# Four exponentials that stay in PSUM: steps 89, 91, 93 and 95 of an attention loop on one Trainium2 core

## The chip, the cores and the metric

One core of one Trainium2 chip runs the whole program. The metric is the device time of one execution in microseconds (us), smaller is better. The engines are TensorE (PE: matmuls, and PEld: loading their stationary operand), VectorE (DVE), ScalarE (ACT), GpSimd (POOL) and SyncE (SP, which issues most DMAs). SBUF is the working memory, PSUM the memory that matmuls write to.

## What is computed

Three blocks in a row, of which the change touches the first:

```python
# attention, batch 2, 8 heads, 768 tokens, head size 64; a query sees keys of its own cluster only
scores = np.where(mask, q @ k.T / 8, -1e9)
attn = np.exp(scores - scores.max(-1)); attn /= attn.sum(-1)
x = attn @ v
# then: Fourier mixing over tokens and channels, layer norm, a ReLU MLP (512 -> 2048 -> 512)
# then: an MLP with a convolution along the tokens and a sigmoid gate (512 -> 1024 -> 512)
```

## The kernel before

**The attention loop.** There are 16 heads of 6 tiles with 128 keys each, so 96 steps; a step n has all 768 queries of one tile. For a step, `score_exp` (L556) makes the scores t in PSUM with four matmuls and ScalarE writes their exponential p (128x768, f32) to SBUF. To keep precision, p is handed on as two 16-bit parts in one tile p16: `prob_hi` (L568) casts p to f16, `prob_lo` (L575) subtracts that part from p again. `attn_v` (L582) then multiplies both parts with v, in 18 small matmuls, of which the first two read the high part only and the other 16 need the low part as well.

**Who does what.** The cast is ScalarE's except in even steps above 87 and in step 95, where it is VectorE's. The subtraction is VectorE's in the steps of `LO_ON_DVE` (L24), which hold the odd steps from 87 on, and GpSimd's in the others. So in the last steps VectorE casts 88, 90, 92, 94 and 95 and subtracts 89, 91, 93 and 95, and GpSimd subtracts 88, 90, 92 and 94.

**Order and buffers.** Every engine takes its instructions in the order of the program. The loop at L739 does in pass n: the row maxima of step n+8 (none after step 95), the cast of step n-1, scores and exponential of step n, the subtraction of step n-1, the product with v of step n-3, and then extra work that tables (`pre`, `aft`, `post`, `fill`) hang into the pass: layer norm of the first half (`un`), the weights of the first MLP step (`firstEH`, `firstEL`, `firstYsH`, `firstYsL`), a small conversion for later (`cw`, `craw`, L898). Scores, row maxima and transposes take turns in three PSUM slots of two banks (`slot`, L318). p has three buffers, p16 four. In the last steps t91 takes the slot of t89, t94 that of t91, t95 that of t92, and t93 that of a transpose (`unT`).

**After the loop.** The first MLP starts (L882). Its matmuls (`up`, `acc`; L78 to L80) stand on TensorE behind the last product with v, and VectorE's conversions and splits of the weights (L281 to L286, L780, L795) stand behind the scaling of the last attention output (L598 to L603), which needs that product too.

Of the kernel before, what the change touches and what calls it, by code (L numbers as in the profile page):

```python
# [10 lines left out]
F32 = mybir.dt.float32  # L11
# [4 lines left out]
AF = mybir.ActivationFunctionType  # L16
# [4 lines left out]
B, H, S, D = 2, 8, 768, 64  # L21

DFT_LOADS = (20, 32)
LO_ON_DVE = {n for n in range(87) if n % 12 in (1, 2, 7, 11)} | set(range(87, 96, 2))  # L24

AHEAD = 4
AHEAD_STEPS = [12 * q + n for q in range(4) for n in (17, 17, 18, 18, 22)]
C = 16
DM = 512
DFF1, DFF2 = 2048, 1024  # L30
# [12 lines left out]
def tile_net(ctx, tc, qk, v, cen, w12, w34, conv, dft, odd, out):  # L43
    nc = tc.nc
    V, A, G, T = nc.vector, nc.scalar, nc.gpsimd, nc.tensor
# [16 lines left out]
    cbias = cp.tile([128, 1], F32, name="cbias")  # L62
    V.memset(cbias, float(P_SHIFT * np.log(2.0)))

    def pool(ctx_, name, bufs=1, side="left"):
        return ctx_.enter_context(tc.tile_pool(name=name, bufs=bufs, side=side, reuse_waits="tile"))
# [168 lines left out]
    def norm(b, bank, lp):  # L235

        X = U[:, 6 * b:6 * b + 6, :]
        stats, ys, os = {}, {}, {}

        def stat(t):  # L240
            if b not in uns:
                uns[b] = up_[b].tile([128, 2, 4, S], F32R, tag="un", bufs=1, name=f"un{b}")
            st = lp.tile([128, 6], F32, tag="st", bufs=2, name=f"st{b}{t}")
            V.bn_stats(st, X[:, t])
            mv = lp.tile([128, 2], F32, tag="mv", bufs=3, name=f"mv{b}{t}")
            V.bn_aggr(mv, st)
            rs = lp.tile([128, 1], F32, tag="rs", bufs=3, name=f"rs{b}{t}")
            V.tensor_scalar(rs, mv[:, 1:2], 1e-6, None, ALU.add)
            stats[t] = (mv, rs)

        def root(t):
            rs = stats[t][1]
            G.tensor_tensor(rs, rs, half[:, 2:3], ALU.pow)

        def scale(t):
            mv, rs = stats[t]
            y = ys[t] = lp.tile([128, DM], F32, tag="y", bufs=1, name=f"y{b}{t}")
            V.tensor_scalar(y, X[:, t], mv[:, 0:1], rs, ALU.subtract, ALU.mult)

        def swap(t):  # L260
            o = os[t] = bank(f"unT{b}{t}").rearrange("p (c n) -> p c n", c=4)
            for c in range(4):
                T.transpose(o[:, c], ys[t][:, 128 * c:128 * c + 128], ident)
            A.copy(uns[b][:, 0, :, 128 * t:128 * t + 128], o)

        def low(t):
            tk = slice(128 * t, 128 * t + 128)
            V.tensor_sub(uns[b][:, 1, :, tk], os[t], f32(uns[b][:, 0, :, tk]))

        return stat, root, scale, swap, low  # L270
# [4 lines left out]
    def from64(dst, raw):  # L275


        w0, w1 = (raw.rearrange("p (n t) -> p n t", t=2)[:, :, i] for i in range(2))
        d = dst.bitcast(I32)
        return (  # L280
            lambda: V.tensor_scalar(d, w1, 3, 0x3FFFFFFF, ALU.logical_shift_left, ALU.bitwise_and),  # L281
            lambda: V.scalar_tensor_tensor(d, w1, -0x40000000, d, ALU.bitwise_and, ALU.bitwise_or),
            lambda: A.activation(f32(w1), f32(w1), AF.Square),
            lambda: V.scalar_tensor_tensor(dst.bitcast(U32), w0.bitcast(U32), 29, dst.bitcast(U32),
                                           ALU.logical_shift_right, ALU.bitwise_or),
            lambda: V.scalar_tensor_tensor(dst, f32(w1), LEAST, dst, ALU.is_ge, ALU.mult),  # L286
        )
# [22 lines left out]
    with ExitStack() as actx:  # L310
        ap = pool(actx, "ap")
# [6 lines left out]
        def slot(name):  # L318
            turn[0] = (turn[0] + 1) % 3
            return ps.tile([128, 2, 512], F32, tag=f"s{turn[0]}", bufs=1, name=name)  # L320
# [37 lines left out]
        t = slot("warm_up")  # L358
# [22 lines left out]
        A.copy(W[64:128, :, 16:32], pwv[:, :, 1])  # L381
        desc = ep.tile([128, C], F16, name="desc")
        for c in range(C):
            G.memset(desc[:, c:c + 1], float(C - c))
        V16s = []
        for i in range(2):
            t = ap.tile([128, NT, 2, 130], F16, name=f"V16_{i}")
# [10 lines left out]
        def prep_sims(m):  # L398
            raw = raws[m]
            sm = sims[m] = first_bank("sim1") if m == 1 else slot(f"sim{m}")[:, 0]  # L400
            for t in range(12):
# [4 lines left out]
            V.tensor_reduce(mx, sv, AX.X, ALU.max)  # L406
            eq = eqs[m] = ep.tile([128, 24, C], F16, tag="eq", bufs=1, name=f"eq{m}")
            V.tensor_tensor(eq.rearrange("p (h g) c -> p h g c", h=2), sv,
                            mx.unsqueeze(3).to_broadcast([128, 2, 12, C]), ALU.is_equal)

        def prep_first(m, eng=G):
            eng.tensor_tensor(eqs[m], eqs[m], desc.unsqueeze(1).to_broadcast([128, 24, C]), ALU.mult)

# [140 lines left out]
        probs, p32s = {}, {}  # L554

        def score_exp(n):  # L556
            h, i = n // 6, n % 6
            X, Y = Xs[h % 3], Ys[h % 3]
            t = slot(f"t{n}")
            sl = slice(128 * i, 128 * i + 128)  # L560
            for c in range(2):
                T.matmul(t[:, c, 0:384], X[:, 1, sl], X[:, 0, 384 * c:384 * c + 384], start=True, stop=False)  # L562
            for c in range(2):
                T.matmul(t[:, c, 0:384], Y[0:98, 1, sl], Y[0:98, 0, 384 * c:384 * c + 384], start=False, stop=True)  # L564
            p = p32s[n] = ap.tile([128, S], F32, tag="p", bufs=3, name=f"p{n}")
            A.activation(p.rearrange("p (c n) -> p c n", c=2), t[:, :, 0:384], AF.Exp, bias=cbias, scale=0.125)  # L566

        def prob_hi(n):  # L568
            p16 = probs[n] = ap.tile([128, 2, S], F16, tag="p16", bufs=4, name=f"p16_{n}")
            if n > 87 and n % 2 == 0 or n == 95:  # L570
                V.tensor_copy(p16[:, 0], p32s[n])
            else:
                A.copy(p16[:, 0], p32s[n])  # L573

        def prob_lo(n):  # L575
            p, p16 = p32s.pop(n), probs[n]
            eng = V if n in LO_ON_DVE else G
            eng.tensor_sub(p16[:, 1], p, p16[:, 0])  # L578

        avs, ds = {}, {}  # L580

# [27 lines left out]
        def at(where, step, *f):  # L609
            where.setdefault(step, []).append(f)  # L610
# [50 lines left out]
        stat, root, scale, swap, low = norm(0, lambda name: slot(name)[:, 0], dp)  # L661
        for i, t in enumerate((0, 3, 1, 4, 2, 5)):
            n = 72 + 3 * i
# [8 lines left out]
        def ahead_start(q):  # L672
# [6 lines left out]
            dst = ahead[q] = t[:, 2560 + 512 * q:3072 + 512 * q]  # L679
            for n, op in zip(AHEAD_STEPS[5 * q:], from64(dst, raw)):  # L680
                at(aft, n, op)
# [9 lines left out]
        for q in range(AHEAD):  # L691
            at(pre, AHEAD_STEPS[5 * q] - 3, ahead_start, q)
            at(pre, AHEAD_STEPS[5 * q + 4] + 1, ahead_store, q)
        for f in range(2):
# [44 lines left out]
        for n in range(-LEAD, 6 * NH + 10):  # L739
            for f in pre.get(n, []):  # L740
                f[0](*f[1:])
            score_max(n + LEAD, mid.get(n, []))
            if 0 <= n - 1 < 6 * NH:
                prob_hi(n - 1)
            if 0 <= n < 6 * NH:
                score_exp(n)
            if 0 <= n - 1 < 6 * NH:
                prob_lo(n - 1)
            if 0 <= n - LAG < 6 * NH:
                attn_v(n - LAG)  # L750
            for f in aft.get(n, []) + post.get(n, []) + fill.get(n, []):
                f[0](*f[1:])
            if n in DFT_LOADS:
                i = DFT_LOADS.index(n)
                G.dma_start(out=DC[:, i], in_=dft[:, i])
            if n == DFT_LOADS[1] + 1:
                G.dma_start(out=OD, in_=odd)
            if n == 6 * NH - 10:
                ectx.close()
                wst.append(pool(ctx, "wst0", side="right"))  # L760
                cvs.append(pool(ctx, "cv", side="right"))
# [219 lines left out]
```

## Time and profile before

| | |
|---|---|
| median of 3 runs | 752.48 us (751.13 to 2342.31) |
| the profiled execution | 750.55 us, of which its span is 748.8 us |
| TensorE busy | 698.7 us, 93% of the span |
| VectorE busy | 536.4 us, 72% |
| ScalarE busy | 345.9 us, 46% |
| GpSimd busy | 271.2 us, 36% |
| the last steps, from the exponential of step 89 to the first matmul of the MLP | 282.6 to 302.0 us |

One of the three runs, 2342.31 us, is far from the other two, 751.13 and 752.48. Shares of the span are averages over stages with different limits; the views below are cut to the last steps of the loop and to what follows them. In a timeline a row is one instruction (or several that follow each other); the bracket at its end says how long the engine was idle before it and which instruction's end released it.

### The profile page before, as it was taken

To read this page: it belongs to the slowest core of one execution; us is meant where nothing else is said; L and a number is where in the kernel's file an instruction comes from. 1 tells how busy PE (TensorE), PEld (TensorE's weight loads), DVE (VectorE), ACT (ScalarE), POOL (GpSimd) and SP (SyncE) were. 2 spreads that over 40 slices of the span, in tenths; PEclk is the share of its full clock that TensorE was granted. 3 is DMA by queue.
4 is the path that set the end of the run, shared out by engine and by line. 5 is a ranking of instruction groups with operands and counts; after the bars stand their busy time and mean duration, and the time that the engine had idled before them with its cause. 6 is when DMAs were issued, how large, how long until landed. Compare 5 with 4: busy or idle time off the path is not lost.

```text
span 748.8 us, 12517 instructions
## 1 busy us (share of the span) xinstructions
PE 698.7 (93%) x5090; PEld 623.2 (83%) x5090; DVE 536.4 (72%) x754; ACT 345.9 (46%) x492; POOL 271.2 (36%) x189
## 2 busy tenths in 40 slices
PE   8898999897998996989999999999999999999996
PEld 6787788786897885878988899999999788898984
DVE  7778989679977998999379937765111268777664
ACT  3576868586466685334234433433222233333321
POOL 8154644455244544131041003222232154443441
PEclk9999999999799999899999999999999999999999
DMA  7637678462533431214104321430000000002002
GB/s 219 173 78 209 184 196 251 107 196 59 157 71 79 92 116 59 98 71 169 57 0 169 116 109 57 168 113 1 1 0 1 1 0 1 1 1 84 1 1 84
DMA packets 19937, 66.47 MB, mean 89 GB/s; under 512 B 2868, under 2 KB 5928, under 8 KB 16808
## 3 DMA queue, kind: packets, MB, share of 16 engines
q1 hardware_dynamic: 19448, 61.93, 28.5%
q0 software_dynamic: 432, 3.75, 1.5%
q8 instruction: 40, 0.66, 0.3%
q14 instruction: 17, 0.14, 0.1%
HBM read 40.94 MB, written 5.77 MB: 62 GB/s over the span
## 4 chain that ended last, share of the span: by engine, by line
PE 48%; DVE 34%; ACT 5%; DMA 4%; POOL 4%; issue 3%; SPq 1%; POOLq 0%; DVEq 0%
PE up L78 5%; DVE m L533 5%; PE up L80 5%; PE up L79 5%; PE acc L80 5%; PE acc L78 5%; PE acc L79 5%; DVE gH L814 5%; DMA vraw<-v 3%; POOL cv L812 3%; PE av L590 3%; PE t L562 2%; DVE cv L809 2%; PE s L528 2%; DVE cv L810 2%
## 5 line engine op out<-in xcount | busy, mean ns | idle before, releaser
L578 POOL TENSOR_TENSOR p<-p,p 128x768 f16<-128x768 f32 x61 | 109.7, 1802 | 115.4 <-ACT p L573 81.7
L566 ACT ACTIVATE p<-t,cbias 128x768 f32<-128x768 f32 x96 | 86.2, 898 | 54.1 <-PE t L564 44.3
L533 DVE TENSOR_REDUCE m<-s 128x1 f32<-128x768 f32 x96 | 90.1, 943 | 13.1 <-PE s L530 6.7
L80 PE MATMUL up<-un,wla 128*128 128x384 f32 x248 | 83.9, 339 | 1.6 <-DVE wla L780 1.6
L78 PE MATMUL up<-un,wha 128*128 128x384 f32 x248 | 84.1, 339 | 0.7 <-DVE YsL L178 0.5
L780 POOL TENSOR_TENSOR wla<-wa,wha 128x1024 fp32r<-128x1024 f32 x16 | 38.5, 2404 | 126.6 <-ACT wha L778 126.6
L79 PE MATMUL up<-un,wha 128*128 128x384 f32 x248 | 83.9, 338 | 0.0
L795 DVE SCALAR_TENSOR_TENSOR hL<-up,hH 128x384 fp32r<-128x384 f32 x62 | 34.2, 552 | 65.6 <-ACT hH L794 65.4
L590 PEld LDWEIGHTS <-p 128*128 128x128 f16 x1728 | 61.1, 100 | 21.6 <-issue 15.4
L590 PE MATMUL av<-V,p 128*128 128x65 f16 x1728 | 73.2, 197 | 5.4 <-POOL p L578 3.6
L573 ACT CAST p<-p 128x768 f16<-128x768 f32 x91 | 75.5, 830 | 1.5
L78 PE MATMUL acc<-wha,hH 128*128 128x512 f32 x186 | 73.7, 396 | 0.0
L80 PE MATMUL acc<-wha,hL 128*128 128x512 f32 x186 | 72.7, 391 | 0.0
L79 PE MATMUL acc<-wla,hH 128*128 128x512 f32 x186 | 72.5, 390 | 0.0
L562 PE MATMUL t<-X 128*128 128x384 f32 x192 | 55.6, 371 | 16.8 <-DVE m L533 14.2
L794 ACT ACTIVATE hH<-up 128x384 fp32r<-128x384 f32 x62 | 30.4, 490 | 75.0 <-PE up L80 74.9
L528 PE MATMUL s<-X 128*128 128x384 f32 x192 | 57.0, 379 | 5.9 <-DVE m L533 4.7
L814 DVE CAST gH<-cv 128x768 fp32r<-128x768 f32 x16 | 35.3, 2209 | 31.3 <-POOL cv L812 31.3
L778 ACT CAST wha<-wa 128x1024 fp32r<-128x1024 f32 x31 | 32.5, 1048 | 52.2 <-PE acc L80 46.3
L812 POOL TENSOR_TENSOR cv<-cv,h 128x768 f32<-128x768 f32 x16 | 25.4, 1590 | 78.1 <-ACT cv L811 78.1
L562 PEld LDWEIGHTS t<-X 128*128 128x128 f32 x192 | 31.9, 193 | 25.1 <-DVE m L533 15.8
L530 PE MATMUL s<-Y 96*128 96x384 f32 x192 | 50.6, 345 | 1.2 <-DMA Y<-G 1.2
(311 smaller groups left out, 1652.0 us busy)
## 6 DMA issues: line engine op xcount, KB each, us to landing
rawa<-w SPq DMA_DIRECT2D x14, 1024.0 KB
rawb<-w SPq DMA_DIRECT2D x8, 1024.0 KB
raw<-qk SPq DMA_DIRECT2D x7, 768.0 KB
X<-G SPq DMA_DIRECT2D x14, 384.0 KB
Y<-G SPq DMA_DIRECT2D x14, 384.0 KB
DC<-dft POOLq DMA_DIRECT2D x2, 1671.0 KB, 7.1
vraw<-v SPq DMA_DIRECT2D x8, 384.0 KB
out<-y SPq DMA_DIRECT2D x12, 256.0 KB
```

Source lines behind the costliest of these rows:

```text
L78: T.matmul(o, sH, mH, start=start, stop=False)
L79: T.matmul(o, sH, mL, start=False, stop=False)
L80: T.matmul(o, sL, mH, start=False, stop=stop)
L528: T.matmul(t[:, c, 0:384], X[:, 0, sl], X[:, 1, 384 * c:384 * c + 384], start=True, stop=False)
L530: T.matmul(t[:, c, 0:384], Y[0:96, 0, sl], Y[0:96, 1, 384 * c:384 * c + 384], start=False, stop=True)
L533: V.tensor_reduce(m6s[h][:, i:i + 1], t[:, :, 0:384], AX.XY, ALU.max, negate=True)
L562: T.matmul(t[:, c, 0:384], X[:, 1, sl], X[:, 0, 384 * c:384 * c + 384], start=True, stop=False)
L566: A.activation(p.rearrange("p (c n) -> p c n", c=2), t[:, :, 0:384], AF.Exp, bias=cbias, scale=0.125)
L573: A.copy(p16[:, 0], p32s[n])
L578: eng.tensor_sub(p16[:, 1], p, p16[:, 0])
L590: T.matmul(o, p16[:, k, 128 * j:128 * j + 128], v16[:, i, h % 2, 65 * part:65 * part + 65], start=(i + j + k + part == 0), stop=(i == 5), ...
L814: V.tensor_copy(g[0], t)
```

## The change

The exponentials of steps 89, 91, 93 and 95 (`IN_PLACE`) are not written to a buffer p in SBUF but back over their own scores in PSUM. ScalarE casts them from there, in step 95 too, where VectorE did it before. VectorE subtracts with the exponential read from PSUM and the high part read from SBUF. The even steps and everything up to step 88 stay as they were; step 87 keeps its engines.

```diff
-LO_ON_DVE = {n for n in range(87) if n % 12 in (1, 2, 7, 11)} | set(range(87, 96, 2))
+LO_ON_DVE = {n for n in range(87) if n % 12 in (1, 2, 7, 11)} | {87}
+IN_PLACE = range(89, 96, 2)
...
-            p = p32s[n] = ap.tile([128, S], F32, tag="p", bufs=3, name=f"p{n}")
-            A.activation(p.rearrange("p (c n) -> p c n", c=2), t[:, :, 0:384], AF.Exp, bias=cbias, scale=0.125)
+            if n in IN_PLACE:
+                p = p32s[n] = t[:, :, 0:384]
+            else:
+                p = p32s[n] = ap.tile([128, S], F32, tag="p", bufs=3, name=f"p{n}")
+                p = halves(p)
+            A.activation(p, t[:, :, 0:384], AF.Exp, bias=cbias, scale=0.125)
+
+        def halves(x):
+            return x.rearrange("p (c n) -> p c n", c=2)
 
         def prob_hi(n):
             p16 = probs[n] = ap.tile([128, 2, S], F16, tag="p16", bufs=4, name=f"p16_{n}")
-            if n > 87 and n % 2 == 0 or n == 95:
+            if n in IN_PLACE:
+                A.copy(halves(p16[:, 0]), p32s[n])
+            elif n > 87:
                 V.tensor_copy(p16[:, 0], p32s[n])
             else:
                 A.copy(p16[:, 0], p32s[n])
...
-            eng.tensor_sub(p16[:, 1], p, p16[:, 0])
+            if n in IN_PLACE:
+                V.tensor_sub(halves(p16[:, 1]), p, halves(p16[:, 0]))
+            else:
+                eng.tensor_sub(p16[:, 1], p, p16[:, 0])
```

What this does to the order is seen at two places. The rows name the line, the operation, what is written and read (t91 are the scores of step 91, p91 its exponential in SBUF, p16_91 its two parts), and which engines it waits for. ScalarE, exponentials and casts of steps 91 to 95, before:

```order
L566 ACTIVATE p91_4229<-t91_4224,cbias_72 128x768 [waits PE_49,Pool_49]
L573 CAST p16_91_4250<-p91_4229 128x768 [waits Activation_49]
L566 ACTIVATE p92_4257<-t92_4252,cbias_72 128x768 [waits PE_49]
L566 ACTIVATE p93_4289<-t93_4284,cbias_72 128x768 [waits PE_49,Pool_49]
L573 CAST p16_93_4314<-p93_4289 128x768 [waits Activation_49]
L566 ACTIVATE p94_4321<-t94_4316,cbias_72 128x768 [waits DVE_49,PE_49]
L566 ACTIVATE p95_4350<-t95_4345,cbias_72 128x768 [waits PE_49,Pool_49]
L778 CAST wha0_1_4497<-wa1_4119 128x1024 [waits DMAHW5_49,DMAHW0_49]
```

The same place of the changed kernel (its lines stand some 2 to 14 further down):

```order
L572 ACTIVATE t91_4223<-t91_4223,cbias_72 128x2x384 [waits PE_49]
L580 CAST p16_91_4248<-t91_4223 128x768 [waits Activation_49]
L572 ACTIVATE p92_4255<-t92_4250,cbias_72 128x768 [waits PE_49]
L572 ACTIVATE t93_4282<-t93_4282,cbias_72 128x2x384 [waits DVE_49,PE_49]
L580 CAST p16_93_4311<-t93_4282 128x768 [waits Activation_49]
L572 ACTIVATE p94_4318<-t94_4313,cbias_72 128x768 [waits PE_49,Pool_49]
L572 ACTIVATE t95_4342<-t95_4342,cbias_72 128x2x384 [waits PE_49]
L580 CAST p16_95_4369<-t95_4342 128x768 [waits DVE_49,Activation_49]
```

The exponentials of 91, 93 and 95 no longer wait for GpSimd, and the cast of step 95 has come to the end of the row.

VectorE, the last instructions of the loop, before:

```order
L578 TENSOR_TENSOR p16_93_4314<-p93_4289,p16_93_4314 128x768 [waits Activation_49]
L603 SCALAR_TENSOR_TENSOR U_68<-av14_4085,vsc7_3641,d14_4278 128x6x64 [waits DVE_49]
L571 CAST p16_94_4343<-p94_4321 128x768 [waits Activation_49,Pool_49]
L705 CAST firstYsH_4371<-wa0_4067 128x512
L571 CAST p16_95_4373<-p95_4350 128x768 [waits Activation_49]
L578 TENSOR_TENSOR p16_95_4373<-p95_4350,p16_95_4373 128x768 [waits DVE_49]
```

And now:

```order
L590 TENSOR_TENSOR p16_93_4311<-t93_4282,p16_93_4311 128x768 [waits PE_49,Activation_49]
L617 SCALAR_TENSOR_TENSOR U_68<-av14_4085,vsc7_3641,d14_4276 128x6x64 [waits DVE_49]
L582 CAST p16_94_4340<-p94_4318 128x768 [waits Activation_49,Pool_49]
L719 CAST firstYsH_4367<-wa0_4067 128x512
L590 TENSOR_TENSOR p16_95_4369<-t95_4342,p16_95_4369 128x768 [waits PE_49,Activation_49]
```

One cast is gone, and the two subtractions read t93 and t95 in the place of p93 and p95.

On TensorE only two waits change. The first matmul of t91, and that of t94, waited for ScalarE (the exponential that emptied the slot); now they wait for VectorE (the subtraction that still reads it).

## Rows read from the trace of the kernel before

**Rows 1.** Busy time in stretches; last columns: granted clock, DMA share, GB/s.

```profile
core 0: us, PE busy (x) PEld busy (x) DVE busy (x) ACT busy (x) POOL busy (x), PEclk, DMA share, GB/s
295.00:300.00 5.00, 2.63 (x54) 2.10 (x54) 4.96 (x6) 1.84 (x2) 3.11 (x3) 0.90 0.01 3
302.00:304.00 2.00, 2.00 (x10) 2.00 (x8) 1.72 (x5) 0.00 (x0) 0.00 (x0) 0.50 0.00 0
304.00:306.00 2.00, 2.00 (x8) 2.00 (x8) 2.00 (x3) 0.00 (x0) 0.00 (x0) 0.54 0.00 0
310.00:320.00 10.00, 10.00 (x53) 9.20 (x52) 9.99 (x12) 4.39 (x6) 3.03 (x3) 1.00 0.59 212
```

**Rows 2.** TensorE's waits, 275 to 303 us: total us, times, longest.

```profile
PE av L590 <- POOL p L578: 3.6, 3, 1.6
PE av L590 <- DVE p L578: 1.4, 1, 1.4
```

**Rows 3.** Timeline of VectorE: start us, us, instruction [idle before].

```profile
278.09 0.94 DVE L533 TENSOR_REDUCE m<-s 128x1 f32<-128x768 f32 x1
278.95 0.94 DVE L578 TENSOR_TENSOR p<-p,p 128x768 f16<-128x768 f32 x1
...
284.42 1.97 DVE L578 TENSOR_TENSOR p<-p,p 128x768 f16<-128x768 f32 x1 [0.35 <-ACT p L573]
...
289.92 2.09 DVE L578 TENSOR_TENSOR p<-p,p 128x768 f16<-128x768 f32 x1 [0.51 <-ACT p L573]
...
292.01 0.41 DVE L705 CAST firstEH<-wa 128x512 fp32r<-128x512 f32 x1
...
293.48 2.40 DVE L578 TENSOR_TENSOR p<-p,p 128x768 f16<-128x768 f32 x1
...
296.33 0.55 DVE L571 CAST p<-p 128x768 f16<-128x768 f32 x1
...
297.13 1.99 DVE L571 CAST p<-p 128x768 f16<-128x768 f32 x1
299.15 1.90 DVE L578 TENSOR_TENSOR p<-p,p 128x768 f16<-128x768 f32 x1
```

**Rows 4.** Timeline of GpSimd, the subtractions of steps 90, 92 and 94.

```profile
289.56 1.65 POOL L578 TENSOR_TENSOR p<-p,p 128x768 f16<-128x768 f32 x1 [3.98 <-DVE p L571]
292.97 2.09 POOL L578 TENSOR_TENSOR p<-p,p 128x768 f16<-128x768 f32 x1 [1.77 <-DVE p L571]
296.95 1.75 POOL L578 TENSOR_TENSOR p<-p,p 128x768 f16<-128x768 f32 x1 [1.89 <-DVE p L571]
```

**Rows 5.** One subtraction of VectorE and one of GpSimd in the first MLP.

```profile
527.60 0.56 DVE L795 SCALAR_TENSOR_TENSOR hL<-up,hH 128x384 fp32r<-128x384 f32 x1 [5.70 <-ACT hH L794]
...
526.08 2.40 POOL L780 TENSOR_TENSOR wla<-wa,wha 128x1024 fp32r<-128x1024 f32 x1 [5.92 <-ACT wha L778]
```

**Rows 6.** Timeline of ScalarE: cast 91, exponentials 93 and 95, others.

```profile
286.73 0.22 ACT L283 ACTIVATE craw<-craw 128x24 f32<-128x24 f32 x1 [2.34 <-DVE cw L282]
...
289.05 0.83 ACT L573 CAST p<-p 128x768 f16<-128x768 f32 x1
...
291.24 0.90 ACT L566 ACTIVATE p<-t,cbias 128x768 f32<-128x768 f32 x1 [0.55 <-POOL p L578]
...
295.10 0.90 ACT L566 ACTIVATE p<-t,cbias 128x768 f32<-128x768 f32 x1 [1.29 <-POOL p L578]
295.90 1.04 ACT L778 CAST wha<-wa 128x1024 fp32r<-128x1024 f32 x1
```

**Rows 7.** Timeline of TensorE: scores of step 91, and the end of the loop.

```profile
285.03 0.59 PE L562 MATMUL t<-X 128*128 128x384 f32 x2
285.46 0.52 PE L564 MATMUL t<-Y 98*128 98x384 f32 x2
...
301.11 1.06 PE L590 MATMUL av<-V,p 128*128 128x65 f16 x16 [1.36 <-DVE p L578]
```

**Rows 8.** Timeline of VectorE after the loop: its one idle time, 303 to 345 us.

```profile
308.76 0.56 DVE L795 SCALAR_TENSOR_TENSOR firste<-up,firste 128x384 fp32r<-128x384 f32 x1 [0.43 <-ACT firste L794]
```

## Prediction

> **What bounds the kernel now.** I read the page first, then the busy time in stretches around the last steps, then TensorE's waits there, then the timelines of the engines side by side. [...] TensorE waits for the parts of the exponentials: three times for GpSimd's subtraction, once, at the very end, for VectorE's [rows 2]. So the end of the loop hangs on a chain of casts and subtractions.
>
> The timeline of VectorE shows what is wrong with that chain. A subtraction takes 0.94 us when alone, but 1.97, 2.09, 2.40 and 1.90 in steps 89, 91, 93 and 95; the cast of step 95 takes 1.99 where that of 94 takes 0.55 [rows 3]. Beside GpSimd's rows the pattern is plain: step 91 starts at 289.92, while GpSimd works from 289.56 to 291.21, and ends at 292.01, 0.80 after GpSimd; step 93 ends at 295.88, 0.82 after GpSimd's 295.06; the cast of 95 ends at 299.12, 0.42 after 298.70 [rows 3, 4]. These instructions of VectorE read SBUF alone, and they stand still while GpSimd's runs. One that reads PSUM does not: in the first MLP a subtraction out of PSUM, 384 columns, runs from 527.60 to 528.16, wholly inside a GpSimd subtraction (526.08 to 528.48), and takes 0.56 [rows 5]. Had it been held it would have ended after 528.48.
>
> Two further waits: the exponentials of steps 93 and 95 stand 0.55 and 1.29 us idle for GpSimd, since their buffer p is still being read [rows 6].
>
> After the loop VectorE is the bound: 9.99 of 10 us between 310 and 320 [rows 1], with one idle time of 0.43 us up to 345 [rows 8]. It starts there when the last product with v is through. What the loop ends earlier, the MLP starts earlier.
>
> **The prices.** *Subtraction out of PSUM*, 768 columns: nearest is a reduction reading 768 columns of PSUM, 0.94; from below also 0.94 (the SBUF subtraction alone) [rows 3], from above twice the 384-column row, 1.12 [rows 5]. I take 0.95. *Exponential written to PSUM*: no row of ScalarE writes PSUM. It reads the same columns as before, 0.90; from below 0.83, the cast, from above 1.04, a cast of a third more columns [rows 6]. I take 0.90. *Cast out of PSUM*: between 0.83 and 0.90, the same columns read from SBUF and from PSUM [rows 6]; I take 0.85, with 1.04 as the far end. The far ends together (0.17 + 0.14 + 0.19) on steps 91, 93 and 95 would take back at most 1.5 us.
>
> [...]
>
> **The walk through the last steps**, each time set against its row.
>
> Step 89. Its subtraction starts at 284.42 as before and ends at 285.37 instead of 286.39: 1.02 earlier [rows 3]. Behind it on VectorE stand the small conversions, for which ScalarE's instruction at 286.73 waits [rows 6]; the exponential of step 90 stands behind that one. All of ScalarE's work up to the cast of 91 comes 1.02 earlier: that cast at 288.03, ending at 288.87 [rows 6].
>
> The new wait: t91 takes over the slot of t89 and now stands on TensorE until 285.4 instead of starting at 285.03, and the products of step 88 stand behind it; 0.4 late. Its four matmuls end 0.95 later [rows 7], at 286.4, while ScalarE comes to that exponential only at 287.1 (289.05 less 0.90 less 1.02). The cover is 0.7 us; without it the 0.4 would be paid.
>
> Step 91. The subtraction runs from 288.9 to 289.85 instead of ending at 292.01: 2.2 earlier. GpSimd's step 90 is released by a cast that comes 1.02 earlier: 288.54 to 290.19 [rows 4]. `firstEH`, next on VectorE, reads SBUF and so stands until 290.19: 1.82 earlier than its 292.01 [rows 3]. With it move the cast of 92 and GpSimd's step 92: 291.15 to 293.24 [rows 4].
>
> Step 93. Its exponential has no buffer to wait for. On ScalarE it follows that of 92: 288.87 + 0.90 + 0.90 = 290.7, and the cast is done by 291.55. VectorE comes to the subtraction at 293.48 less 1.82 = 291.66 and ends it at 292.6 instead of 295.88: 3.3 earlier. The cast of 94, 0.45 later in the row before [rows 3], would start at 293.05, meets GpSimd's step 92 and ends 0.42 after it, at 293.66. Step 94 on GpSimd then runs from 293.73 to 295.48 instead of 296.95 to 298.70 [rows 4]: 3.2 earlier. t94 waits for the subtraction of 91, at 289.85, but stands behind products that GpSimd's step 90 holds until 290.2, so that wait is covered.
>
> Step 95. TensorE has t94 from 290.75 and t95, after the products of 91, from about 292.1; so the exponential of 95 runs from 293.1 to 294.0, the cast on ScalarE to 294.9, the subtraction to 295.85 instead of 301.05: 5.2 earlier. The cast that goes from VectorE takes 1.99 us of waiting with it.
>
> TensorE. The last 16 products of step 94 start at 295.53, those of 95 follow. At half clock 16 take 1.06 [rows 7], at full clock half of that; so the loop ends at about 296.65 instead of 302.17: **5.5 us earlier**. With TensorE denser I expect the clock to stay at 1.0; then the first `up` matmuls don't run at half clock and the 0.43 idle of VectorE goes too [rows 8]. More the clock doesn't give, since VectorE bounds what follows. Sum: 5.5 + 0.4 = 5.9 us.
>
> The profiled execution has 750.55 us, so 744.65. The two close runs, 751.13 and 752.48, lie 1.25 above it in the mean; I add that: **745.9 us**.
>
> **Rivals.** *VectorE is still held.* If a subtraction that reads one operand from PSUM also stands behind GpSimd, steps 89, 91 and 93 end as before, and GpSimd's step 94 at 298.70. Only the cast of 95 is gone from VectorE, and its subtraction ends at 298.70 + 0.80 = 299.5 instead of 301.05: 1.55 us, giving 750.25. The row of the MLP speaks against it [rows 5].
>
> *The MLP does not follow rigidly.* GpSimd works 3.03 of the 10 us after 310 [rows 1], on SBUF, and each meeting with VectorE can cost 1.0 to 1.5 us (2.40 less 0.94) or be missed. TensorE is then earlier against VectorE, and the meetings fall elsewhere. One more or one fewer gives 747.4 or 744.4.
>
> *TensorE's clock gives more.* The granted clock is 0.50 from 302 and 0.54 in the mean from 304 to 306 [rows 1], so some 3.8 us of `up` run at half clock. If VectorE were not the bound after the loop, they would shrink by 1.9 us, in which the 0.43 is contained: 750.55 - 5.5 - 1.9 + 1.25 = 744.4.
>
> *Slower: the slots.* A score slot is now free only after the subtraction. If reading PSUM beside ScalarE and TensorE slowed it, steps 91, 93 and 95 pay it in a row, and t91 and t94 wait with them. Three times the surplus must exceed 5.9, so it decides from 0.95 + 2.0 = 2.9 us each. At 3.3 us the time would be 753. No PSUM row is near that.
>
> **How the numbers follow.** The walk as forecast, 743.8 to 747.5: 0.70. Part of the gain lost (prices at their far ends, one meeting more, or VectorE held), 747.5 to 750.5: 0.16. More than forecast, below 743.8: 0.08. Slower or no gain, above 750.5: 0.06. The range 743.0 to 750.5 leaves out a little over 1 in 10. A measurement of this kernel tells about 2%, 15 us, from no change; the whole gain is 0.8%. So faster by over 2%: 0.01; within 2%: 0.98; slower by over 2%: 0.01.
>
> **What would show it.** Right: four subtractions of about 0.95 us on VectorE beside running GpSimd rows; no wait of the exponentials 93 and 95 for GpSimd; no cast of 95 on VectorE; the first `up` matmul near 296.6; a granted clock of 1.0 through 302. Wrong: subtractions near 2 us again (VectorE held), an exponential well over 1 us, a wait of t91 that ends in ScalarE being idle, or VectorE idle or longer behind GpSimd between 297 and 345.

## The result and the profile after

The changed kernel takes **741.71 us** in the median of four runs (740.73 to 743.33), the kernel before beside it 751.81. The ratio is 0.9881 (95% interval 0.9853 to 0.9908), so the gain is real but under 2%. Forecast were 745.9 us and a range of 743.0 to 750.5: the time is 1.3 us below the range. (One run of before, 2342.31 us, is left out of the ratio.)

The profiled execution of after has a span of 741.5 us, 7.3 less than before. In the last steps it looks as forecast. Busy time in the same stretches as [rows 1], after:

```profile
core 0: us, PE busy (x) PEld busy (x) DVE busy (x) ACT busy (x) POOL busy (x), PEclk, DMA share, GB/s
295.00:300.00 5.00, 4.78 (x55) 4.78 (x56) 4.03 (x8) 1.13 (x3) 1.40 (x2) 1.00 0.00 0
304.00:306.00 2.00, 2.00 (x13) 2.00 (x12) 2.00 (x4) 2.00 (x3) 0.00 (x0) 1.00 0.44 82
```

TensorE works 4.78 of the 5 us from 295, where it worked 2.63 (from 296.28 on this is the MLP already), and its granted clock is 1.00 from 295 to 300 and from 304 to 306 instead of 0.50 to 0.54 behind the loop [rows 1]. Of its 5.0 us of waits for the parts of the exponentials [rows 2] two are left:

```profile
PE av L604 <- POOL p L592: 2.0, 2, 1.0
```

The timeline of VectorE after (start, us, instruction, idle time before it):

```profile
284.01 0.96 DVE L590 TENSOR_TENSOR p<-t,p 128x768 f16<-128x768 f32 x1 [0.29 <-ACT p L580]
...
288.64 0.96 DVE L590 TENSOR_TENSOR p<-t,p 128x768 f16<-128x768 f32 x1 [0.45 <-ACT p L580]
...
289.58 0.68 DVE L719 CAST firstEH<-wa 128x512 fp32r<-128x512 f32 x1
...
291.32 0.94 DVE L590 TENSOR_TENSOR p<-t,p 128x768 f16<-128x768 f32 x1
...
292.71 0.61 DVE L582 CAST p<-p 128x768 f16<-128x768 f32 x1
...
294.62 0.96 DVE L590 TENSOR_TENSOR p<-t,p 128x768 f16<-128x768 f32 x1 [0.96 <-ACT p L580]
296.48 0.16 DVE L612 TENSOR_SCALAR d<-av 128x6 f32<-128x6 f32 x1 [0.91 <-PE av L604]
```

And GpSimd's:

```profile
283.34 1.89 POOL L592 TENSOR_TENSOR p<-p,p 128x768 f16<-128x768 f32 x1 [2.09 <-DVE p L582]
288.33 1.65 POOL L592 TENSOR_TENSOR p<-p,p 128x768 f16<-128x768 f32 x1 [3.11 <-DVE p L582]
290.81 2.10 POOL L592 TENSOR_TENSOR p<-p,p 128x768 f16<-128x768 f32 x1 [0.83 <-DVE p L582]
293.40 1.76 POOL L592 TENSOR_TENSOR p<-p,p 128x768 f16<-128x768 f32 x1 [0.49 <-DVE p L582]
```

The four subtractions of steps 89, 91, 93 and 95 take 0.94 to 0.96 us where they took 1.97, 2.09, 2.40 and 1.90 [rows 3], each while GpSimd is at work. The casts, which still read SBUF alone, still end only after it: `firstEH` at 290.26, 0.28 us after GpSimd's step 90 (289.98), the cast from 292.71 at 293.32, 0.41 after its step 92 (292.91). ScalarE after, whose rows writing to t answer the price that the trace of before did not show [rows 6]:

```profile
282.27 0.88 ACT L572 ACTIVATE t<-t,cbias 128x768 f32<-128x768 f32 x1 [1.45 <-DVE p L592]
283.18 0.80 ACT L580 CAST p<-t 128x768 f16<-128x768 f32 x1
...
289.30 0.88 ACT L572 ACTIVATE t<-t,cbias 128x768 f32<-128x768 f32 x1
290.20 0.80 ACT L580 CAST p<-t 128x768 f16<-128x768 f32 x1
...
292.88 0.88 ACT L572 ACTIVATE t<-t,cbias 128x768 f32<-128x768 f32 x1 [0.39 <-PE t L566]
```

And TensorE, the new wait of t91 and the end of the loop, where before had [rows 7]:

```profile
285.02 0.62 PE L564 MATMUL t<-X 128*128 128x384 f32 x2
...
295.22 1.22 PE L604 MATMUL av<-V,p 128*128 128x65 f16 x34 [0.96 <-POOL p L592]
296.28 0.42 PE L80 MATMUL up<-un,firstEH 128*128 128x384 f32 x1
```

The MLP begins at 296.28 instead of 301.99. To see what of that is the change's, the program is cut into five stretches at rows that each trace has: the start of step 89's exponential, the first `up` matmul, the first and the last cast gH of the gated MLP, the end of the span. Times in us, one profiled execution each; the kernels below are those of the experiments.

| kernel | step 89 at | **tail**: 89 to first `up` | to first gH | to last gH | to the end | span |
|---|---|---|---|---|---|---|
| before | 282.62 | **19.37** | 307.99 | 127.32 | 11.50 | 748.8 |
| before, again | 279.32 | **19.36** | 307.84 | 127.46 | 11.72 | 745.7 |
| after | 282.27 | **14.01** | 307.40 | 127.35 | 10.47 | 741.5 |
| after, again | 283.98 | **14.01** | 307.43 | 127.36 | 10.52 | 743.3 |
| cast 95 and fourth buffer | 284.48 | **17.84** | 307.72 | 127.34 | 10.42 | 747.8 |
| cast 95 only | 279.06 | **18.00** | 307.82 | 127.33 | 11.69 | 743.9 |
| buffer only | 280.45 | **19.36** | 307.75 | 127.29 | 10.45 | 745.3 |
| in place up to 93 | 280.82 | **15.81** | 307.89 | 127.31 | 11.47 | 743.3 |
| before, matmuls in the tail | 282.74 | **19.00** | 307.35 | 127.34 | 11.47 | 747.9 |
| before, matmuls at the end | 283.55 | **19.37** | 308.03 | 127.30 | 10.55 | 748.8 |
| before, later v maximum | 277.24 | **19.36** | 307.57 | 127.39 | 10.44 | 742.0 |
| after, later v maximum | 280.06 | **14.00** | 307.41 | 127.30 | 11.73 | 740.5 |
| after, late craw | 280.15 | **13.10** | 308.26 | 127.70 | 10.49 | 739.7 |
| after, both moves | 278.31 | **13.10** | 308.20 | 127.79 | 10.40 | 737.8 |

The tail repeats to 0.01 us, so one profile measures it. It is 5.36 us shorter after; the stretch behind it is 0.41 to 0.59 shorter. That is the change. The other two differences, 1.0 to 1.2 us at the end and the start of step 89, have to be explained.

### The profile page after: what moved, and what is told of

Read it like the earlier page. It is cut to its first block, busy times and chain, and to the rows that moved or that the text cites. A ratio compares the mean times of both kernels' runs of the same rounds, so it can differ in the third digit from the quotient of the medians.

```text
span 741.5 us, 12519 instructions
## 1 busy us (share of the span) xinstructions
PE 694.9 (94%) x5090; PEld 618.4 (83%) x5090; DVE 531.4 (72%) x753; ACT 346.8 (47%) x493; POOL 269.6 (36%) x189
## 4 chain that ended last, share of the span: by engine, by line
PE 45%; DVE 35%; DMA 5%; POOL 5%; ACT 4%; issue 3%; SPq 1%; POOLq 0%; DVEq 0%
DVE m L535 5%; PE acc L82 5%; DVE gH L828 5%; PE acc L80 5%; PE acc L81 5%; PE up L82 5%; PE up L80 5%; PE up L81 5%; DMA vraw<-v 4%; POOL cv L826 3%; PE av L604 3%; DVE cv L823 2%; DVE cv L824 2%; PE t L564 2%; PE s L530 2%
## 5 line engine op out<-in xcount | busy, mean ns | idle before, releaser
L572 ACT ACTIVATE p<-t,cbias 128x768 f32<-128x768 f32 x92 | 82.7, 899 | 51.7 <-PE t L566 50.9
L584 ACT CAST p<-p 128x768 f16<-128x768 f32 x88 | 73.0, 830 | 1.4
L604 PE MATMUL av<-V,p 128*128 128x65 f16 x1728 | 71.7, 196 | 2.0 <-POOL p L592 2.0
L566 PE MATMUL t<-Y 98*128 98x384 f32 x192 | 50.9, 347 | 0.1
```

What stands on the lines that cost most here:

```text
L572: A.activation(p, t[:, :, 0:384], AF.Exp, bias=cbias, scale=0.125)
L604: T.matmul(o, p16[:, k, 128 * j:128 * j + 128], v16[:, i, h % 2, 65 * part:65 * part + 65], start=(i + j + k + part == 0), stop=(i == 5), ...
```

## The experiments

**Both kernels once more.** No edit; 23 runs of before beside them.

> The kernel before once more, nothing changed: how much its runs differ, and where. The forecast was 745.9 us, 5.9 below the profiled execution, and the changed kernel came out at 741.7, with one run at 743.3 and three at 740.7 to 742.1. Theory A, the rest lies outside the change: the runs of the two kernels differ before step 89 and in the last 10 us, in stretches with the granted clock at half, and these differ from run to run. Then the runs here spread over at least 747 to 752 us with a mean clock between 0.979 and 0.99. Theory B, the change itself brings 9 us in every run: all runs here lie between 750 and 752.5 with a clock near 0.979.

> The changed kernel once more. Theory A: runs between 740 and 745 us, the difference from the kernel before in the mean of the runs near 6 to 7; in the trace, the time from the start of the exponential of step 89 to the first matmul of the MLP is 14.0 us again (19.4 before). Theory B: 740 to 743 in every run, 9 us or more below the kernel before.

Measured: before 749.25 us (746.01 to 753.05; ratio to the 23 runs, 750.55 in the median, 0.9983, interval 0.9964 to 1.0002), after 744.27 (740.35 to 745.27; ratio 0.9905, 0.9875 to 0.9935). The gain is 6.3 us here and was 10.1 at first, with the same tails. Runs of before alone spread over 9 us, 746.01 to 755.08, and its two profiles come to step 89 at 282.62 and 279.32. So part of the first measurement's gain lay outside of the tail, as theory A has it.

**All but PSUM.** The cast of step 95 goes to ScalarE and p gets a fourth buffer; exponentials stay in SBUF.

```diff
-            if n > 87 and n % 2 == 0 or n == 95:
+            if n > 87 and n % 2 == 0:
                 V.tensor_copy(p16[:, 0], p32s[n])
...
-                p = p32s[n] = ap.tile([128, S], F32, tag="p", bufs=3, name=f"p{n}")
+                p = p32s[n] = ap.tile([128, S], F32, tag="p", bufs=4, name=f"p{n}")
```

> The kernel before with everything that the change brings except the PSUM operand: step 95 is cast by ScalarE, and p has four buffers in SBUF, so the exponentials of 93 and 95 need not wait for GpSimd. Theory A, VectorE's subtraction is held while GpSimd runs and is set free by the PSUM operand: the subtractions of 89, 91, 93 and 95 take 1.9 to 2.4 us as before, and the stretch from the exponential of 89 to the first matmul of the MLP shrinks from 19.4 by 1.6 to some 17.8 us; total 1.5 to 2.5 below the kernel before. Rival, the buffers and the place of the cast make the difference: the stretch shrinks to 14 or 15 us and the total is 5 us or more lower.

Measured: tail 17.84 us, 747.57 us (745.46 to 750.27), ratio 0.995 (0.9928 to 0.9972). The four subtractions, read from SBUF, are as long as before:

```profile
286.28 1.97 DVE L578 TENSOR_TENSOR p<-p,p 128x768 f16<-128x768 f32 x1 [0.36 <-ACT p L573]
...
291.79 2.09 DVE L578 TENSOR_TENSOR p<-p,p 128x768 f16<-128x768 f32 x1 [0.51 <-ACT p L573]
...
295.34 2.40 DVE L578 TENSOR_TENSOR p<-p,p 128x768 f16<-128x768 f32 x1
...
298.99 2.39 DVE L578 TENSOR_TENSOR p<-p,p 128x768 f16<-128x768 f32 x1
```

1.53 us of the tail's 5.36 are had without PSUM, 3.83 are not. The whole time is 3.0 us below the runs of before, over the 1.5 to 2.5 expected; that is within the spread seen above.

**The two halves of that, each alone** (the two hunks above, one at a time).

> The kernel before with one part of the change: the cast of step 95 goes from VectorE to ScalarE, all else stays, the three buffers of p too. Measure: from the start of the exponential of step 89 to the first matmul of the MLP (19.37 us before, 14.01 after, 17.84 with this cast and a fourth buffer of p). Theory: the cast alone is what the run with the fourth buffer gained, since VectorE's subtraction of step 95 is released by the end of GpSimd's of step 94 in both, so 17.8 us. Rival, that the exponentials of 93 and 95, which wait for a buffer, count too: 18.5 us or more here.

> The kernel before with a fourth buffer for p and nothing else. Same measure. Theory: the waits of the exponentials 93 and 95 for GpSimd (0.55 and 1.29 us) go, but the cast of 95 stands behind VectorE's held subtraction of step 93 anyway, so nothing is won: 19.4 us. Rival, the buffers count: 18.1 us (1.29 less).

Measured: 18.00 us with the cast alone, 19.36 with the buffer alone. With the buffer the exponentials of 93 and 95 no longer wait for GpSimd, but nothing comes of it. VectorE with the buffer alone, steps 93 and 95:

```profile
291.30 2.40 DVE L578 TENSOR_TENSOR p<-p,p 128x768 f16<-128x768 f32 x1
...
294.95 1.99 DVE L571 CAST p<-p 128x768 f16<-128x768 f32 x1
296.97 1.90 DVE L578 TENSOR_TENSOR p<-p,p 128x768 f16<-128x768 f32 x1
```

The durations are those of [rows 3]: the exponentials were early enough, and VectorE, held by GpSimd, was the bound. With the cast alone (VectorE, then GpSimd's step 94):

```profile
293.57 2.39 DVE L578 TENSOR_TENSOR p<-p,p 128x768 f16<-128x768 f32 x1
```
```profile
293.39 1.75 POOL L578 TENSOR_TENSOR p<-p,p 128x768 f16<-128x768 f32 x1 [1.89 <-DVE p L571]
```

The subtraction of 95 then stands behind GpSimd's step 94 and ends 0.82 us after it (295.96 and 295.14), as the forecast's rival "VectorE is still held" had it. The 0.16 us by which its tail is longer than with both hunks lies in the last 34 products: to the first `up` matmul they take 1.86 us here (295.20 to 297.06) and 1.70 there (300.62 to 302.32), where the granted clock is 0.72 in the mean from 300 to 302. That it is 0.50 all through here is an estimate: before, 16 products take 0.88 us to the first `up` matmul (301.11 to 301.99) with the clock at 0.50 from 300 to 302, and 34/16 of that is 1.87.

**In place up to step 93.** After, with step 95 as before.

```diff
-LO_ON_DVE = {n for n in range(87) if n % 12 in (1, 2, 7, 11)} | {87}
+LO_ON_DVE = {n for n in range(87) if n % 12 in (1, 2, 7, 11)} | {87, 95}
...
-IN_PLACE = range(89, 96, 2)
+IN_PLACE = range(89, 95, 2)
```

> The kernel after, with steps 89, 91 and 93 in place and step 95 as in the kernel before (exponential in SBUF, cast and subtraction on VectorE). Same measure. Theory, VectorE's two instructions of step 95 are held by GpSimd again, the cast behind the subtraction of 94 and the subtraction behind firstYsL: 15.4 to 16.2 us, against 14.0 with 95 in place and 19.4 before. Rival, only the steps up to 93 count: 14.0 to 14.5.

Measured: tail 15.81 us. VectorE's two instructions of step 95, and GpSimd's beside them:

```profile
292.42 1.71 DVE L582 CAST p<-p 128x768 f16<-128x768 f32 x1 [0.21 <-ACT p L572]
294.17 1.90 DVE L592 TENSOR_TENSOR p<-p,p 128x768 f16<-128x768 f32 x1
```
```profile
291.95 1.76 POOL L592 TENSOR_TENSOR p<-p,p 128x768 f16<-128x768 f32 x1 [0.50 <-DVE p L582]
293.68 1.57 POOL L717 TENSOR_TENSOR firstYsL<-wa,firstYsH 128x512 fp32r<-128x512 f32 x1
```

The cast ends 0.42 after the first, the subtraction 0.82 after the second. So steps 89 to 93 in place are worth 3.56 us and step 95 another 1.80. It is the same in each step of these runs: a cast or a subtraction of VectorE that reads SBUF alone and meets a running subtraction of GpSimd ends only after it, the casts by 0.28 to 0.42 us, the subtractions by 0.80 to 0.82; one that reads an operand from PSUM doesn't wait, 0.94 to 0.96 us. The rest of the trace of after bounds this. It needs nothing of these four steps: the eight subtractions of the MLP out of PSUM (hL, 384 columns) that begin while GpSimd works take 0.56 us and end before it does. Where VectorE began first, it was GpSimd that took longer: VectorE's `firstEL` begins at 290.75 and takes 0.64, and GpSimd's step 92, from 290.81, takes 2.10 where step 90 took 1.65. And not all that reads SBUF alone is held: six reductions of a v tile in SBUF begin while GpSimd subtracts and take 0.93 to 0.95 us, such as this one, which ends at 8.75, before GpSimd's 9.57:

```profile
7.81 0.94 DVE L489 TENSOR_REDUCE vsc<-vraw 128x1 f32<-128x768 f32 x1
```
```profile
7.66 1.91 POOL L463 TENSOR_TENSOR G<-raw,G 128x768 fp32r<-128x768 f32 x1
```

**TensorE's clock in the tail.** Before, with work that nobody reads.

```diff
+                if n - LAG in (94, 95):
+                    d = slot(f"keep{n}")[:, 0]
+                    for _ in range(4):
+                        T.matmul(d, probs[n - LAG][:, 0, 0:128], probs[n - LAG][:, 0, 0:512], start=True, stop=True)
                 attn_v(n - LAG)
```

> The kernel before with four extra matmuls of 512 columns (on the f16 parts of p, into a score slot, nobody reads them) ahead of the products of step 94 and again of 95, so that TensorE is less idle there. Two measures: the tail, exponential of 89 to first matmul of the MLP (19.37 before), and from that matmul to the first cast gH of the gated MLP (308.0 and 307.8 in two profiles of before, 307.4 in two of after). Theory, the half clock costs the 16 last products 0.5 us and VectorE's 0.43 us idle behind it the rest: with the clock at 1.0 the tail is 18.8 us and the stretch behind it 307.4 us. Rival, the clock costs nothing there: 19.4 us or more and 307.9 us.

Measured: tail 19.00, behind it 307.35 us. The granted clock stays up where it was 0.50 [rows 1]:

```profile
300.00:302.00 2.00, 1.23 (x21) 0.96 (x20) 1.24 (x2) 0.00 (x0) 0.36 (x1) 1.00 0.00 0
302.00:304.00 2.00, 2.00 (x13) 2.00 (x13) 1.93 (x5) 0.00 (x0) 0.00 (x0) 1.00 0.00 0
```

So the half clock cost before 0.37 us in the tail, which is part of the 5.36, and 0.5 to 0.6 behind it, which covers the 0.41 to 0.59 that after wins there. The table agrees: leaving out the two kernels with the late craw, the four profiles in which the `up` matmuls behind the first take 0.34 us each from the start (after, at a clock of 1.00 from 298 to 300) have 307.35 to 307.43 us to the first gH, the eight in which they take 0.52 there (before, at 0.50 from 302 to 304), "in place up to 93" from the third on, have 307.57 to 308.03.

**TensorE's clock at the end.** Before, with six matmuls in TensorE's last idle time.

```diff
+        if n == 8 * B - 1:
+            d = up_bank("keep")
+            for _ in range(6):
+                T.matmul(d, ws[1, 1, 7][2][:, 0:128], ws[1, 1, 7][2], start=True, stop=True)
         down(1, n // 8, n % 8, side)
```

> The kernel before with six extra matmuls of 512 columns, that nobody reads, ahead of the last 18 products of the gated MLP, where TensorE is 1.58 us idle for VectorE's last cast gH. Measure: from that last cast to the end of the span (11.50 and 11.72 us in two profiles of before, where the granted clock falls to 0.50 in those products, 10.47 and 10.52 in two of after, where it does not). Theory, the 1.1 us that after wins there is TensorE's clock alone: 10.4 to 10.6 us here with the tail of the loop as before (19.4). Rival, the end is shorter for another reason (the stores): 11.5 us.

Measured: 10.55 us to the end. TensorE's row of two microseconds in the last products, the second profile of before, then after, then before with the extra matmuls:

```profile
736.00:738.00 2.00, 2.00 (x6) 1.52 (x6) 0.30 (x1) 0.59 (x1) 0.00 (x0) 0.50 0.06 25
```
```profile
734.00:736.00 2.00, 2.00 (x10) 1.64 (x9) 0.63 (x1) 0.59 (x1) 0.00 (x0) 1.00 0.61 223
```
```profile
740.00:742.00 2.00, 2.00 (x9) 1.64 (x10) 0.69 (x1) 0.73 (x2) 0.00 (x0) 1.00 0.06 20
```

The last 1.0 to 1.2 us are the clock alone: 6 matmuls in 2 us at 0.50, 9 or 10 at 1.00. But it is no property of the change. In the table the long end stands with before, with the matmuls in the tail, with the cast alone, with "in place up to 93" and with one variant of after; the short one with after, with its two late-craw variants and with three variants of before that leave the end alone. TensorE's idle time ahead of it is the same 1.58 us in before and 1.59 in after. What decides it stays open.

**The wait for v.** The two profiles of before part between steps 40 and 42. There VectorE waits for a loaded tile of v; the second profile of before, then after:

```profile
133.86 0.95 DVE L487 TENSOR_REDUCE vsc<-vraw 128x1 f32<-128x768 f32 x1 [2.66 <-DMA vraw<-v]
```
```profile
135.57 0.95 DVE L489 TENSOR_REDUCE vsc<-vraw 128x1 f32<-128x768 f32 x1 [4.83 <-DMA vraw<-v]
```

In the first profile of before it is 4.88. TensorE waits 2.64 us behind it, and from 140 to 142 us its clock is 0.50. The reduction was therefore moved two passes later, in both kernels.

```diff
-            at(fill, k + 16, v_max, m)
-            at(mid, k + 18, v_turn, m)
+            at(fill, k + 18, v_max, m)
+            at(mid, k + 20, v_turn, m)
             for i in range(4):
-                at(aft, k + 18, v_step, m, i)
+                at(aft, k + 20, v_step, m, i)
```

> The kernel after with VectorE's reduction of a loaded v tile two steps later, with what hangs on it. In the profiles so far VectorE waits for that load four times, 9.7 us in sum in the profile of before that came fast to step 89 (279.3 us) and 12.1 in the one that came late (282.6); in the late ones TensorE is 2.6 us idle behind it and then at half clock. Theory, the runs of one kernel differ mainly by this wait, and it is no part of the change: without it the exponential of step 89 starts at 276 to 279.5 us, the time is 737 to 741 us, and the tail stays 14.0. Rival, the spread is elsewhere: step 89 at 280 to 284 us and 742 to 745 us as for after.

> The same move of the reduction in the kernel before, so that the change can be measured with that wait out of the way. Theory: 745 to 748 us, and between this run and the kernel after with the same move lie the 5.4 us of the tail, 0.5 us behind it and, where the end of the program runs at half clock, 1.1 us: 6 to 7 us. Rival, the change gained more by something outside of the tail, as the medians of the first measurement (10.1 us) say: 9 us or more between the two.

Measured: before with the move 746.65 us (743.79 to 749.02; ratio to 15 runs of before 0.995, 0.9926 to 0.9975), after with it 742.25 (740.40 to 743.67; 0.9891, 0.9865 to 0.9918). The waits for v are 0 in both. Before won 3.6 us; after won nothing that shows, its ratio lies between the two it had without the move. The time of after, 742.25, lies outside of the 737 to 741 expected and where its rival had it. The theory was half right. The spread between steps 40 and 42 is gone: the three profiles with the move have step 54's exponential at 169.27 to 169.62 us, while before's two have it at 169.44 and 172.56. But step 89 still came at 277.24 and at 280.06, against 276 to 279.5 expected. These two part between steps 56 and 61, with the same work and the same idle time. TensorE's stretch from 178 us and the idle time ahead of it, before with the move, then after with it:

```profile
178.00:182.00 4.00, 4.00 (x55) 3.54 (x55) 4.00 (x11) 2.88 (x5) 1.61 (x2) 1.00 0.02 5
```
```profile
177.59 0.58 PE L562 MATMUL t<-X 128*128 128x384 f32 x2 [2.02 <-DVE vsc L500]
```
```profile
178.00:182.00 4.00, 4.00 (x33) 3.43 (x32) 3.07 (x8) 1.46 (x3) 0.62 (x1) 0.62 0.02 4
```
```profile
177.47 0.87 PE L564 MATMUL t<-X 128*128 128x384 f32 x2 [2.03 <-DVE vsc L502]
```

After 2.02 us of idle time the clock stays at 1.00, after 2.03 us it falls: 55 matmuls in 4 us or 33. At the next such idle time, 2.49 and 2.48 us, it falls in both, but from 190 to 194 us it is at 0.99 in the one and at 0.50 in the other. After the first the kernel after is 1.42 us behind, after both the 2.82 by which it comes to step 89 later. Between the two kernels lie 4.4 us in the median, under the 6 to 7 expected. In their profiles it wins 5.36 in the tail and 0.16 behind it and loses 1.29 at the end, where the kernel after now has the long one, 11.73: 4.2 from step 89 on. The 2.82 before step 89 go the other way, so the two spans differ by 1.5 only.

**The small conversion.** `craw` and `cw` (L898 before) are loaded and converted in the first MLP instead of between steps 89 and 90.

```diff
-    craw = wp.tile([128, 48], I32, tag="craw", bufs=1, name="craw")
-    nc.sync.dma_start(out=craw.bitcast(I64), in_=conv)
...
             if (g, f) == (1, 9):
+                craw = cvs[0].tile([128, 2048], I32, tag="raw64", bufs=2, name="craw")[:, 0:48]
+                nc.sync.dma_start(out=craw.bitcast(I64), in_=conv)
                 for op in from64(cw, craw):
```

> The changed kernel with the small conversion of the convolution's weights (cw, craw) moved from the end of the loop into the first MLP, where it has time. In the changed kernel ScalarE is idle 1.53 us before craw, with the exponential of step 90 queued behind it. Theory A, the loop's end is still the chain of casts and subtractions, and this wait is on it: the exponential of 90 comes 1.6 us earlier, that of 91 0.9, GpSimd's step 90 1.5, and the stretch from the exponential of 89 to the MLP shrinks from 14.0 to about 12.8; total 1.2 us lower. Rival, TensorE or ScalarE now set the pace there: the stretch stays within 0.3 us of 14.0.

> The kernel after with the later reduction and with the small conversion of craw and cw moved out of the loop's tail into the first MLP. Theory: both gains add up, since they lie in different stretches: tail 13.1 us as with the later conversion alone, time about 1 us below that of the kernel after with the later reduction alone. Rival, one eats the other: the same time as that kernel.

Measured, on after alone: tail 13.10 us, 743.39 us (741.49 to 748.08; ratio 0.9912, 0.9879 to 0.9945). The tail is 0.91 shorter, near the expected 1.2, but the stretches behind it are 0.83 and 0.34 longer than in "after, again" (308.26 against 307.43, 127.70 against 127.36). Why stays open; it takes the gain back. With both moves: 739.85 us (739.59 to 740.95; ratio 0.9863, 0.9835 to 0.9890), the fastest kernel here and 2.4 below the kernel after with the later reduction, where 1 was expected. But the table gives it from step 89 to the end 459.5 us and after 459.2: what it has ahead of after it has before step 89.

## Why the prediction was right, and where it failed

**The bound and the walk were right.** Times of after are put on the clock of before by the 0.35 us with which it came to step 89 earlier. The subtraction of 89 ends at 285.32 (forecast 285.37), t91 starts at 285.37 (285.4), the subtraction of 91 runs from 288.99 (288.9), that of 93 from 291.67 (291.66), the cast of 94 to 293.67 (293.66), GpSimd's step 94 from 293.75 (293.73), the exponential of 95 from 293.23 (293.1); the subtraction of 95 ends at 295.93 (295.85), and the last products are through at 296.79 by their row or 296.63 by the next row's start (296.65). Two misses of some 0.14 us cancel in it: the first small conversion meets GpSimd's step 88 and takes 0.38 us instead of 0.16, so that GpSimd's step 90 starts at 288.68 (288.54), and `firstEH` ends 0.28 after that step where the walk has 0.41. The loop ends 5.36 us earlier against 5.5 forecast.

**The prices were right.** Subtraction out of PSUM 0.94 to 0.96 us (0.95), exponential to PSUM 0.88 (0.90), cast from it 0.80 (0.85). Against the 0.94 us of the subtraction out of SBUF alone [rows 3] the one out of PSUM was 0 to 0.02 us longer. The exponential was 0.02 us shorter into PSUM than the 0.90 into SBUF [rows 6]. That the PSUM operand releases VectorE the runs show; why, they don't. The subtractions that met GpSimd took 1.90 to 2.40 us with two inputs in SBUF and 0.94 to 0.96 with one. The cast of 95 has one input, in SBUF, and was held as well (1.99 and 1.71 us).

**The rivals.** "VectorE is still held" did not happen, but its price did, where it was built: 1.53 us with the exponentials in SBUF and the cast on ScalarE (1.55). "The MLP does not follow rigidly" didn't happen either: 307.40 and 307.43 us against 307.84 and 307.99, and most of the difference is VectorE's idle time there, 0.43 us in the first profile of before [rows 8] and none up to 345 us in the first of after; with the clock kept at 1.00 before had 307.35. "TensorE's clock gives more" was right in the kind and wrong in the place: not the start of the MLP but the last products of the program gave 1.0 to 1.2 us more. "Slower: the slots" found no surplus to pay.

**What failed is the last step, from the sum to the time and its range.** 5.9 us was the right size for what the change does: 5.36 and 0.41 to 0.59. The step "I add that: 745.9 us" took everything but the tail and the 0.4 us behind it as fixed, the end of the program too ("More the clock doesn't give"), and the lower end of 743.0 left under 3 us for the rest. Two things lay there. TensorE's clock in the last products fell in before, to 0.50, and stayed at 1.00 in after: 1.0 to 1.2 us, which other kernels lost or kept whatever their tail was. And runs of one kernel spread over 5 to 10 us; the profiles show two sources, a clock that falls or doesn't after idle times of the same length, and a load of v that comes earlier or later, and there are more: the second profile of after is 1.5 us behind its first already at a row maximum at 64.34 us (62.87). Three runs of before, one of them far off, did not show that. The runs of after sort by their mean clock: of all ten, four at 0.993 or more took 740.35 to 742.10 us, six at 0.984 to 0.988 took 743.33 to 745.27. Three of the first measurement's four are of the first kind, so it was in part luck of the draw that it fell below the range; its profiled run, 743.33, lies inside, and so does the median of the ten, 743.5. No execution of after of the first kind was profiled, so where it keeps its clock stays open. The first measurement's 10.1 us hold an estimated 3 us of this spread (10.1 less 5.36, 0.5 and 1.2), the second's 6.3 us are close to the forecast: 750.55 less 5.9 is 744.65, and 744.27 was measured.

## What to carry to other kernels

Where VectorE stands behind GpSimd, look in the trace which of VectorE's instructions end only after GpSimd's: here casts and subtractions that read SBUF alone did, by 0.28 to 0.42 and 0.80 to 0.82 us, reductions of 0.93 to 0.95 us did not. For the subtractions one operand left in PSUM was enough to free them, 0.94 to 0.96 us against 1.90 to 2.40, and it cost 0 to 0.02 us here. Before a wait is called worth its length, ask whether the engine behind it is held anyway: the two waits for a buffer, 1.84 us, were worth nothing alone. And give a forecast of a small gain a range from the spread of the runs, not from the terms of the sum: measure the stretch that changes, it repeats to 0.01 us where the whole time spreads by 1%.

## What the runs showed that was not expected

- After idle times of TensorE of the same length at the same place of the program (2.02 and 2.03 us), the granted clock stayed at 1.00 in one kernel and fell in the other, to 0.62 in the mean of the next 4 us. The 2.82 us by which those two come to step 89 apart arise there and at the next such idle time. Why stays open.
- The clock sorts the runs of before too, but only roughly: of 35, the six with a mean clock of 0.977 or 0.978 took 753.0 to 755.1 us, the seven at 0.986 or above 748.5 to 752.2. The fastest, 746.0, stands at 0.984, one of 753.05 at 0.982, and of the 15 later runs one at 0.978 took 750.4.
- Taking a small load out of the loop's tail made what follows longer: from the first `up` matmul to the first gH 308.26 and 308.20 us, against 307.40 to 307.43 in after.
